# Idle products around the opening transposes, one normalization moved ahead of weight splits, and two tiles' transposes moved inside V

## The chip, the cores and the metric

The kernel runs on one core of a Trainium2 chip. The metric is the time of one execution in microseconds on the device; the time before is the median of three runs. A core has five engines with queues of their own: PE (TensorE, matrix products and transposes), DVE (VectorE), ACT (ScalarE), POOL (GpSimd) and SP (SyncE, which here issues the DMA transfers). Each works through its instructions in order; semaphores tie them together.

## The reference

The program is a block of two layers on x of 2048 rows and 640 columns, in float32. First sliding-window attention with 32 heads of 20, then a gated MLP with a product over the positions:

```python
h = x + _A_ref(_layernorm(x), A_wqkv, A_wo)          # attention, window 256
h2 = h + _B_ref(_layernorm(h), B_w_in, B_w_sp, B_b_sp, B_w_out)
# _A_ref begins with
qkv = (x @ wqkv).reshape(B, S, 3, H, Dh)
```

What matters here is the very beginning: the layer normalization of x and V, the product of normalized x with the 640 columns of wqkv that make v.

## The kernel before

x is cut into 16 tiles of 128 rows (tile 0 to 15). Products are made at about float32 accuracy from operands that are split in two: `hi`, a rounded copy that ACT writes, and `lo`, the rest, `raw - hi`, that DVE or POOL computes. Each product of V is then three: hi·hi, hi·lo and lo·hi.

The kernel opens with the V stage. Its parts, per tile i:

- `load_x(i)`: a DMA of the tile, issued by SP into one of three buffers.
- `ln1(i)` (through `layernorm`, L71 to L83): on DVE the statistics (two at L76, L77, L78), on POOL the reciprocal root as a power (L79), on DVE the normalized tile `xn` (L82). An optional function `between` is called after L79 is issued and before L82, so what it issues on DVE stands between them.
- `turn1(i)`: five transposes on PE (L443), in two banks of PSUM, four and one; ACT copies each bank as hi (L447), DVE subtracts for lo (L448). PSUM banks are taken in turn from a ring of three (`s2_tile`).
- `vgemm(i)`: two halves of 320 columns (j = 0 and 1), in each five steps k of three products (L459, L460, L461), then a copy to `v_sb` on ACT (L462). The profile shows the first half as tile `v`, the second as `bank`; wv's split pieces are `slot` (hi and lo), the transposed x is `xa` (later `xb`).

The weight wv arrives as ten pieces, five for the first 320 columns and five for the other 320, and `split_wv` turns each into hi (ACT, L529) and lo (DVE or POOL, L530). The order of the beginning is written by hand: for DVE, PE and ACT the program's order is the order of execution. It is: `ln1(0)` with the split of the first piece as `between`, splits of the other four pieces of the first half, `turn1(0)`, `ln1(1)`, splits of the second half. Then the loop over tiles: `load_x(i + 3)`, `ln1(i + 2)`, and `vgemm(0)` before `turn1(1)` for i = 0, but `turn1(i + 1)` before `vgemm(i)` for every later i.

After the V stage come the products for q and k, the attention loop, the output projection and the MLP; the change touches none of them.

Of the kernel before, what the change touches and what calls it, by code (L numbers as in the profile page):

```python
# [7 lines left out]
F32 = mybir.dt.float32  # L8
F32R = mybir.dt.float32r
BF16 = mybir.dt.bfloat16  # L10
# [5 lines left out]
P = 128  # L16
# [4 lines left out]
NT = S // P  # L21
KD = D // P
# [12 lines left out]
def block_kernel(ctx, tc, x, wqk, wv, wo, w_in, wsp, bsp, w_out, out):  # L35
    nc = tc.nc
# [4 lines left out]
    def pool(stack, name, **kw):  # L41
        return stack.enter_context(tc.tile_pool(name=name, bufs=1, reuse_waits="tile", **kw))
# [29 lines left out]
    def layernorm(dst, src, n, key, between=None):  # L72
        st, mv = stat_tiles(key)
        hn = n // 2
        for j in range(2):
            nc.vector.bn_stats(out=st[:, j, :], in_=src[:, j * hn:(j + 1) * hn])  # L76
        nc.vector.bn_aggr(out=mv[:, 0:2], in_=st)  # L77
        nc.vector.tensor_scalar(out=mv[:, 2:3], in0=mv[:, 1:2], scalar1=EPS, scalar2=None, op0=OP.add)  # L78
        nc.gpsimd.tensor_tensor(out=mv[:, 3:4], in0=mv[:, 2:3], in1=half, op=OP.pow)  # L79
        if between is not None:  # L80
            between()
        nc.vector.tensor_scalar(out=dst, in0=src, scalar1=mv[:, 0:1], scalar2=mv[:, 3:4],  # L82
                                op0=OP.subtract, op1=OP.mult)  # L83
# [118 lines left out]
    with ExitStack() as ab:  # L202
# [6 lines left out]
        xb = pool(lowx, "xb")  # L209
        xb = [xb.tile([P, CH], F32R, name=f"xb{i}") for i in range(2)]  # L210
# [39 lines left out]
        banks = [ps6.tile([P, 512], F32, name=f"bank{i}") for i in range(6)]  # L250
        ring = {1: banks[2::-1], 2: banks[3:]}

        def s_tile(which):
            ring[which].append(ring[which].pop(0))
            return ring[which][-1]

        def s1_tile():
            return s_tile(1)

        def s2_tile():  # L260
            return s_tile(2)

        def pv_tile(name):
            return psA.tile([P, 512], F32, tag="pv", bufs=2, name=name)
# [158 lines left out]
        if True:  # L423
# [3 lines left out]
            def load_x(i):  # L427
                xts[i] = tmp.tile([P, D], F32, tag="ta", bufs=3, name=f"xt{i}")
                for c in halves if i == 0 else (slice(0, D),):
                    nc.sync.dma_start(xts[i][:, c], x[i * P:(i + 1) * P, c])  # L430

            def ln1(i, between=None):
                xn = tmp.tile([P, D], F32, tag="tb", bufs=2, name=f"xn{i}")
                layernorm(xn, xts.pop(i), D, f"a{i}", between)
                xns[i] = xn

            def turn1(i):
                xn = xns.pop(i)
                c, o = divmod(i, 4)
                for k0, k1 in ((0, 4), (4, KD)):  # L440
                    ps = s2_tile()
                    for k in range(k0, k1):
                        nc.tensor.transpose(ps[:, (k - k0) * P:(k - k0 + 1) * P], xn[:, k * P:(k + 1) * P], ident)  # L443
                    hi = xn_hi[c][:, k0:k1, o * P:(o + 1) * P]
                    lo = xn_lo[c][:, k0:k1, o * P:(o + 1) * P]
                    p3 = ps[:, :(k1 - k0) * P].rearrange("p (k t) -> p k t", k=k1 - k0)
                    nc.scalar.activation(hi, p3, AF.Copy)  # L447
                    nc.vector.tensor_tensor(out=lo, in0=p3, in1=hi.bitcast(F32), op=OP.subtract)  # L448

            def vgemm(i):  # L450
                c, o = divmod(i, 4)
                t0 = o * P
                for j in range(2):
                    ps = s1_tile() if j else pv_tile(f"v{i}_{j}")
                    n0 = j * HD
                    for k in range(KD):
                        hi, lo = xn_hi[c][:, k, t0:t0 + P], xn_lo[c][:, k, t0:t0 + P]
                        wh, wl = wv_hi[:, k, n0:n0 + HD], wv_lo[:, k, n0:n0 + HD]
                        nc.tensor.matmul(ps[:, :HD], hi, wh, start=(k == 0), stop=False)  # L459
                        nc.tensor.matmul(ps[:, :HD], hi, wl, start=False, stop=False)  # L460
                        nc.tensor.matmul(ps[:, :HD], lo, wh, start=False, stop=(k == KD - 1))  # L461
                    nc.scalar.activation(v4[:, i, 16 * j:16 * j + 16, :DH],  # L462
                                         ps[:, :HD].rearrange("p (h c) -> p h c", c=DH), AF.Copy)
# [3 lines left out]
            def load_wqk(m):  # L467
                raws[m] = tmp.tile([P, KD, P], F32, tag="wraw", bufs=4, name=f"wqraw{m}")
                nc.sync.dma_start(raws[m], wqk[m])

            def split_wqk(m):
                raw = raws.pop(m)
                hi = tmp.tile([P, KD, P], F32R, tag="wqh", bufs=4, name=f"wqh{m}")
                lo = tmp.tile([P, KD, P], F32R, tag="wql", bufs=4, name=f"wql{m}")
                nc.scalar.activation(hi, raw, AF.Copy)
                nc.gpsimd.tensor_tensor(out=lo, in0=raw, in1=hi.bitcast(F32), op=OP.subtract)
                wqs[m] = (hi, lo)
# [41 lines left out]
            halves = [slice(0, HD), slice(HD, D)]  # L519
# [8 lines left out]
            def split_wv(k, c, eng):  # L528
                nc.scalar.activation(wv_hi[:, k, c], wv_raw[k][:, c], AF.Copy)  # L529
                eng.tensor_tensor(out=wv_lo[:, k, c], in0=wv_raw[k][:, c], in1=wv_hi[:, k, c].bitcast(F32),  # L530
                                  op=OP.subtract)

            c = halves[0]
            ln1(0, lambda: split_wv(0, c, nc.vector))
            for k in range(1, KD):
                split_wv(k, c, nc.vector if k % 2 == 0 else nc.gpsimd)
            turn1(0)
            ln1(1)
            for k in range(KD):
                split_wv(k, halves[1], nc.gpsimd if k % 2 else nc.vector)  # L540
            for i in range(NT):
                if i + 3 < NT:
                    load_x(i + 3)
                if i + 2 < NT:
                    ln1(i + 2)
                if i == 0:
                    vgemm(0)
                if i + 1 < NT:
                    turn1(i + 1)
                if i >= NT - 6 and i < NT - 2:  # L550
                    load_wqk(i - (NT - 6))
                if i >= NT - 3:
                    split_wqk(i - (NT - 3))
                if i:
                    vgemm(i)
            for j in range(4):
                r = slice(32 * j, 32 * j + 32)
# [646 lines left out]
    n = NT - 2  # L1204
# [34 lines left out]
```

## Time and profile before

| | |
|---|---|
| time before, median of 3 runs | 1129.89 us (1129.07 to 1131.32) |
| the profiled execution, its own time | 1132.75 us |
| its span, first to last instruction | 1130.4 us |
| mean granted TensorE clock over the span | 0.991 |
| 40 slices of the span | 28.3 us each |

The span is what the profile sees; the execution's own time is 2.35 us longer, for what lies around the first and the last instruction. The tables read from left to right: start in us from the span's start, duration, engine, line, operation, written tile <- read tile, and in square brackets how long the engine was idle just before and what ended that. The line numbers are those of the kernel before. The clock column of a stretch is the share of full TensorE clock that was granted, as far as the profile recorded its changes.

### The profile page before, as it was taken

To read this page: it belongs to the slowest core of one execution; us is meant where nothing else is said; L and a number is where in the kernel's file an instruction comes from. 1 tells how busy PE (TensorE), PEld (TensorE's weight loads), DVE (VectorE), ACT (ScalarE), POOL (GpSimd) and SP (SyncE) were. 2 spreads that over 40 slices of the span, in tenths; PEclk is the share of its full clock that TensorE was granted. 3 is DMA by queue.
4 is the path that set the end of the run, shared out by engine and by line. 5 is a ranking of instruction groups with operands and counts; after the bars stand their busy time and mean duration, and the time that the engine had idled before them with its cause. 6 is when DMAs were issued, how large, how long until landed. Compare 5 with 4: busy or idle time off the path is not lost.

```text
span 1130.4 us, 27633 instructions
## 1 busy us (share of the span) xinstructions
PE 1092.4 (97%) x10652; PEld 982.4 (87%) x10652; DVE 739.5 (65%) x2011; ACT 551.1 (49%) x1181; POOL 385.2 (34%) x505
## 2 busy tenths in 40 slices
PE   6999999999999999888999999999999999999998
PEld 6998887668887886788999999999989899999998
DVE  6541222889999997599678478655457974556542
ACT  4333443259999999343366566433336521222210
POOL 3114444457777778365230154000034410000000
PEclk9999999999999999898999999999999999999999
DMA  6212565665666645578555421424341554444331
GB/s 198 70 36 87 167 224 172 199 210 187 220 207 205 205 133 184 169 255 279 207 170 198 152 66 39 137 85 142 118 164 54 170 185 143 124 147 137 109 93 60
DMA packets 84420, 172.61 MB, mean 153 GB/s; under 512 B 11072, under 2 KB 47424, under 8 KB 80448
## 3 DMA queue, kind: packets, MB, share of 16 engines
q1 hardware_dynamic: 81984, 165.60, 45.5%
q10 hardware_dynamic: 2304, 5.24, 1.2%
q8 instruction: 83, 1.36, 0.5%
q14 instruction: 49, 0.40, 0.1%
HBM read 113.25 MB, written 57.11 MB: 151 GB/s over the span
## 4 chain that ended last, share of the span: by engine, by line
PE 72%; DVE 10%; DMA 7%; issue 5%; POOL 4%; SPq 2%; ACT 1%; POOLq 0%; DVEq 0%; ACTq 0%
PE g L1030 20%; PE out_ps L1069 8%; PE pv L395 6%; PE bank L301 5%; PE bank L367 5%; PE wo_ps L92 3%; PE zx L867 2%; PE qk L483 2%; PE qk L485 2%; PE qk L484 2%; PE zv L867 2%; DVE zl L676 2%; DVE aw L676 2%; PE zy L867 1%; POOL sg L502 1%
## 5 line engine op out<-in xcount | busy, mean ns | idle before, releaser
L370 ACT ACTIVATE pt<-bank 128x384 f32<-128x384 f32 (+2 forms) x512 | 200.4, 492 | 9.6 <-PE bank L367 5.0
L1030 PE MATMUL g<-zl,aw 128*128 128x432 f32 x768 | 172.7, 362 | 1.6 <-DVE zl L676 1.3
L682 ACT ACTIVATE aw<-fx 128x512 fp32r<-128x512 f32 (+2 forms) x160 | 92.5, 594 | 156.7 <-PE g L1030 99.4
L313 DVE CUSTOM_DVE_ANT_0 junk<-bank,strip 128x288 bf16<-128x288 f32 x392 | 157.5, 454 | 4.1 <-PE bank L301 1.4
L1030 PEld LDWEIGHTS g<-zl,aw 128*128 128x128 f32 x768 | 144.8, 190 | 9.1 <-DVE zl L676 2.3
L1030 PE MATMUL g<-ze,aw 128*128 128x432 f32 x576 | 134.0, 362 | 4.5 <-DVE row L676 2.5
L395 PE MATMUL pv<-pt,v_sb 128*32 128x192 f32 (+3 forms) x1984 | 127.2, 322 | 3.6 <-POOL pt L372 2.1
L676 DVE TENSOR_TENSOR aw<-fx,aw 128x512 fp32r<-128x512 f32 (+2 forms) x152 | 106.9, 713 | 27.1 <-ACT aw L682 26.3
L1030 PEld LDWEIGHTS g<-ze,aw 128*128 128x128 f32 x576 | 107.1, 188 | 12.4 <-DVE row L676 4.1
L367 PE MATMUL bank<-slot 123*32 123x288 bf16 (+5 forms) x1536 | 106.2, 280 | 1.6 <-ACT pt L370 0.6
L372 POOL TENSOR_SCALAR_AFFINE_SELECT pt<-pt 128x512 f32<-128x512 f32 x128 | 84.4, 659 | 44.9 <-ACT pt L370 44.1
L1069 PE MATMUL out_ps<-wout,y_sp 128*128 128x320 f32 (+1 forms) x630 | 96.2, 309 | 0.4 <-ACT y_sp L125 0.4
L919 PE MATMUL zb<-win,aw 128*128 128x432 f32 x480 | 95.5, 359 | 0.0
L1069 PEld LDWEIGHTS out_ps<-wout,y_sp 128*128 128x128 f32 (+1 forms) x630 | 94.0, 188 | 1.2 <-ACT y_sp L125 0.7
L919 PEld LDWEIGHTS zb<-win,aw 128*128 128x128 f32 x480 | 89.9, 188 | 5.0 <-ACT aw L682 0.4
L301 PE MATMUL bank<-slot 120*32 120x288 bf16 (+2 forms) x1264 | 88.5, 283 | 1.3 <-DVE mcol L313 1.0
L499 DVE TENSOR_TENSOR rest<-qk,sg 128x512 f32<-128x512 f32 x40 | 27.7, 691 | 86.1 <-ACT sg L497 86.0
L375 POOL TENSOR_SCALAR_AFFINE_SELECT pt<-pt 128x512 f32<-128x512 f32 x112 | 72.6, 648 | 0.0
L502 POOL TENSOR_TENSOR sg<-rest,sg 128x512 bf16<-128x512 f32 x40 | 46.6, 1165 | 69.6 <-ACT sg L501 65.8
L395 PEld LDWEIGHTS pv<-pt,v_sb 128*32 128x32 f32 x1984 | 60.0, 110 | 9.5 <-POOL pt L372 4.3
L367 PEld LDWEIGHTS <-slot 123*32 123x32 bf16 x1536 | 53.0, 96 | 16.8 <-issue 5.9
L676 DVE TENSOR_TENSOR row<-g,row 128x432 f32<-128x432 f32 x80 | 47.9, 602 | 29.4 <-PE g L1030 24.1
(190 smaller groups left out, 2169.4 us busy)
## 6 DMA issues: line engine op xcount, KB each, us to landing
fx<-wsp_in SPq DMA_DIRECT2D x32, 512.0 KB
slot<-qk_d SPq DMA_DIRECT2D x72, 200.0 KB
qk_d<-sg SPq DMA_DIRECT2D x32, 384.0 KB
slot<-qk_d SPq DMA_DIRECT2D x72, 160.0 KB
fx<-hn_d SPq DMA_DIRECT2D x32, 320.0 KB
o_d<-ot SPq DMA_DIRECT2D x64, 128.0 KB
z_d<-row SPq DMA_DIRECT2D x18, 432.0 KB
g_d<-row SPq DMA_DIRECT2D x16, 432.0 KB
```

The lines of the kernel that those rows point to most:

```text
L301: nc.tensor.matmul(ps[32 * j:32 * j + 32, :n], part(st, half, 120, 0, hh, q0, 32), part(st, half, 120, 1, hh, lo + skip * j, n), start=Tru ...
L313: nc.vector.tensor_tensor_reduce(out=junk[:, :n], in0=ps[:, :n], in1=keep, scale=1.0, scalar=NEG, op0=OP.add, op1=OP.max, accum_out=m_cols ...
L367: nc.tensor.matmul(ps[32 * i:32 * i + 32, b:e], part(st, half, 123, 1, hh, k0, 32), part(st, half, 123, 0, hh, kb * P + b, e - b), start=T ...
L370: nc.scalar.activation(pt[:, hh, :n], ps[:, :n], AF.Exp, scale=SCALE)
L372: nc.gpsimd.affine_select(out=pt[:, :, :P], in_=pt[:, :, :P], pattern=[[0, 4], [1, P]], base=0, channel_multiplier=-1, compare_op=OP.is_ge ...
L375: nc.gpsimd.affine_select(out=pt[:, :, 256:], in_=pt[:, :, 256:], pattern=[[0, 4], [-1, P]], base=-1, channel_multiplier=1, compare_op=OP. ...
L395: nc.tensor.matmul(ps[32 * hh:32 * hh + 32, a - 512 * c:b - 512 * c], v_sb[:, kb, v0:v0 + 32], pt[:, hh, a - kb * P:b - kb * P], start=fir ...
L676: (eng or nc.vector).tensor_tensor(out=out, in0=a, in1=b, op=op)
L682: nc.scalar.activation(out, a, AF.Copy)
L919: nc.tensor.matmul(b[0][:, :HF], a[t][:, x, kk], win2[0][:, y, kk, h * HF:(h + 1) * HF], start=kk + x + y == 0, stop=kk == KD - 1 and x == 1)
L1030: nc.tensor.matmul(ps, w[m][:, x, k], zc[k][m][:, y], start=start and k + x + y == 0, stop=stop and k == 3 and x == 1, skip_group_check=True)
L1069: nc.tensor.matmul(ps[j][:, :HD], src[:w, a, k, :], e1["wout"][:w, b, k, j * HD:(j + 1) * HD], start=(k == 0 and a + b == 0), stop=(k == K ...
```

## The change

Four things are done.

1. At the start DVE fills a piece of `xb[1]`, not yet in use, with ones, and PE runs 11 products of 128 x 512 on it into `banks[0]`; four more follow `turn1(0)`. Nobody reads their result.
2. `ln1(0)` is issued whole before any split, and `turn1(0)` stands after the third of the first half's five pieces, not after the fifth.
3. In `ln1(1)` the first two pieces of wv's second half are split between the power and the normalization; on DVE that is one remainder ahead of `xn` of tile 1 and two behind.
4. `vgemm` gets a parameter `middle`, called in its second half before step k = 3. For i = 0 and 1 the transposes `turn1(i + 1)` stand there, and `ln1(i + 2)` follows behind `vgemm(i)`. From i = 2 on the loop is as before.

```diff
+        idle = xb[1][:, :256].bitcast(F32)
+        nc.vector.memset(idle, 1.0)
+        idle = idle.bitcast(BF16)
+
+        def idle_products(n):
+            for _ in range(n):
+                nc.tensor.matmul(banks[0], idle[:, :P], idle, start=True, stop=True)
+
+        idle_products(11)
...
-            def vgemm(i):
+            def vgemm(i, js=(0, 1), middle=None):
                 c, o = divmod(i, 4)
                 t0 = o * P
-                for j in range(2):
+                for j in js:
                     ps = s1_tile() if j else pv_tile(f"v{i}_{j}")
                     n0 = j * HD
                     for k in range(KD):
+                        if middle is not None and (j, k) == (1, 3):
+                            middle()
...
-            c = halves[0]
-            ln1(0, lambda: split_wv(0, c, nc.vector))
-            for k in range(1, KD):
-                split_wv(k, c, nc.vector if k % 2 == 0 else nc.gpsimd)
+            def split_half(c, ks):
+                for k in ks:
+                    split_wv(k, c, nc.gpsimd if k % 2 else nc.vector)
+
+            ln1(0)
+            split_half(halves[0], range(3))
             turn1(0)
-            ln1(1)
-            for k in range(KD):
-                split_wv(k, halves[1], nc.gpsimd if k % 2 else nc.vector)
+            idle_products(4)
+            split_half(halves[0], range(3, KD))
+            ln1(1, lambda: split_half(halves[1], range(2)))
+            split_half(halves[1], range(2, KD))
             for i in range(NT):
                 if i + 3 < NT:
                     load_x(i + 3)
+                if i < 2:
+                    vgemm(i, middle=lambda: turn1(i + 1))
                 if i + 2 < NT:
                     ln1(i + 2)
-                if i == 0:
-                    vgemm(0)
-                if i + 1 < NT:
+                if 1 < i < NT - 1:
                     turn1(i + 1)
...
-                if i:
+                if i > 1:
                     vgemm(i)
```

How that moves VectorE's rows, from the normalization of tile 1 to that of tile 3. The digit behind a name is the tile or the piece (`xn1`, `wvraw2`); `slot0_1` is lo of wv, L448 writes lo of the transposed tile. Before:

```order
L82 TENSOR_SCALAR xn1_179<-xt1_141,mva1_181 128x640
L530 TENSOR_TENSOR slot0_1_101<-wvraw0_131,slot0_0_100 128x320
L530 TENSOR_TENSOR slot0_1_101<-wvraw2_133,slot0_0_100 128x320
L530 TENSOR_TENSOR slot0_1_101<-wvraw4_135,slot0_0_100 128x320
L76 BN_STATS sta2_201<-xt2_148 128x6 x2
L77 BN_AGGR mva2_202<-sta2_201 128x2
L78 TENSOR_SCALAR mva2_202<-mva2_202 128x1
L82 TENSOR_SCALAR xn2_200<-xt2_148,mva2_202 128x640
L448 TENSOR_TENSOR xa_91<-bank5_124,xa_91 128x4x128
L448 TENSOR_TENSOR xa_91<-bank3_122,xa_91 128x128
L76 BN_STATS sta3_254<-xt3_198 128x6 x2
```

And with the change, the same engine and stretch:

```order
L542 TENSOR_TENSOR slot0_1_101<-wvraw0_143,slot0_0_100 128x320
L82 TENSOR_SCALAR xn1_195<-xt1_153,mva1_197 128x640
L542 TENSOR_TENSOR slot0_1_101<-wvraw2_145,slot0_0_100 128x320
L542 TENSOR_TENSOR slot0_1_101<-wvraw4_147,slot0_0_100 128x320
L458 TENSOR_TENSOR xa_91<-bank5_124,xa_91 128x4x128
L458 TENSOR_TENSOR xa_91<-bank3_122,xa_91 128x128
L76 BN_STATS sta2_259<-xt2_160 128x6 x2
L77 BN_AGGR mva2_260<-sta2_259 128x2
L78 TENSOR_SCALAR mva2_260<-mva2_260 128x1
L82 TENSOR_SCALAR xn2_258<-xt2_160,mva2_260 128x640
L458 TENSOR_TENSOR xa_91<-bank4_123,xa_91 128x4x128
L458 TENSOR_TENSOR xa_91<-bank5_124,xa_91 128x128
```

The first remainder of the second half moved ahead of `xn1`, and the statistics of tile 2, which stood ahead of tile 1's two subtractions, now stand behind them; those of tile 3 stand behind tile 2's as before, but tile 2's subtractions are now issued from inside V of tile 1. The row after the last is the statistics of tile 3.

On PE, the end of V of tile 1 (`bank1`) and what follows it. Before:

```order
L460 MATMUL bank1_120<-slot0_1_101,xa_91 128x320
L461 MATMUL bank1_120<-slot0_0_100,xa_91 128x320
L443 MATMUL bank3_122<-ident_73,xn3_253 128x128 x4
L443 MATMUL bank4_123<-ident_73,xn3_253 128x128
L459 MATMUL v2_0_324<-slot0_0_100,xa_91 128x320
```

With the change:

```order
L473 MATMUL bank1_120<-slot0_0_100,xa_91 128x320
L453 MATMUL bank4_123<-ident_73,xn2_258 128x128 x4
L453 MATMUL bank5_124<-ident_73,xn2_258 128x128
L471 MATMUL bank1_120<-slot0_0_100,xa_91 128x320
L472 MATMUL bank1_120<-slot0_1_101,xa_91 128x320
L473 MATMUL bank1_120<-slot0_0_100,xa_91 128x320
L471 MATMUL bank1_120<-slot0_0_100,xa_91 128x320
L472 MATMUL bank1_120<-slot0_1_101,xa_91 128x320
L473 MATMUL bank1_120<-slot0_0_100,xa_91 128x320
L453 MATMUL bank3_122<-ident_73,xn3_311 128x128 x4
L453 MATMUL bank4_123<-ident_73,xn3_311 128x128
L471 MATMUL v2_0_340<-slot0_0_100,xa_91 128x320
```

The transposes of tile 2 moved from ahead of V of tile 1 to six products before its end; those of tile 3 stand where they stood, between V of tile 1 and V of tile 2.

## The prediction

> **What bounds the kernel now.** I read the page first (engine totals and the chain that ended last), then the timeline of the opening microseconds, then the same chain in order of time, then clock and busy time in stretches around TensorE's longest waits.
>
> From the page, busy time and the chain's shares:
>
> ```profile
> PE 1092.4 (97%) x10652; PEld 982.4 (87%) x10652; DVE 739.5 (65%) x2011; ACT 551.1 (49%) x1181; POOL 385.2 (34%) x505
> PE 72%; DVE 10%; DMA 7%; issue 5%; POOL 4%; SPq 2%; ACT 1%; POOLq 0%; DVEq 0%; ACTq 0%
> ```
>
> TensorE is the bound and the program is one long chain. The change touches only its first 30 us, so I ask one question: when does the even rhythm of the V stage begin, before and after? What that moment gains or loses goes through to the end. I call V0, V1, V2 the 30 products of tiles 0, 1, 2, and A and B the two halves of wv's columns.
>
> The opening, from the timeline (start, duration, engine, line, what, in brackets the idle time ahead and its releaser):
>
> ```profile
> 0.80 0.20 POOL L60 MEMSET ident<- 128x128 f32 x1 [0.29 <-POOLq L1231]
> 1.86 1.14 POOL L243 MEMSET v_sb<- 128x512 f32 x1
> 4.60 0.57 POOL L79 TENSOR_TENSOR mva<-mva,half 128x1 f32<-128x1 f32 x1 [0.27 <-DVE mva L78]
> 5.19 1.32 ACT L529 ACTIVATE slot<-wvraw 128x320 fp32r<-128x320 f32 x3 [3.11 <-DMA wvraw<-wv_in]
> 5.69 0.49 DVE L530 TENSOR_TENSOR slot<-wvraw,slot 128x320 fp32r<-128x320 f32 x1 [1.17 <-ACT slot L529]
> 6.10 1.27 DVE L82 TENSOR_SCALAR xn<-xt,mva 128x640 f32<-128x640 f32 x1
> 7.43 1.33 PE L443 MATMUL bank<-ident,xn 128*128 128x128 f32 x5 [7.43 <-DVE xn L82]
> 8.58 0.77 ACT L447 ACTIVATE xa<-bank 128x512 fp32r<-128x512 f32 x2 [0.54 <-PE bank L443]
> 9.23 0.64 PE L459 MATMUL v<-slot,xa 128*128 128x320 f32 x1 [0.47 <-ACT xa L447]
> 9.45 2.23 ACT L529 ACTIVATE slot<-wvraw 128x320 fp32r<-128x320 f32 x5
> 10.01 0.88 DVE L76 BATCH_NORM_STATS2 sta<-xt 128x6 f32<-128x320 f32 x2
> 10.43 1.77 POOL L530 TENSOR_TENSOR slot<-wvraw,slot 128x320 fp32r<-128x320 f32 x2 [1.94 <-ACT slot L529]
> 12.16 0.56 POOL L79 TENSOR_TENSOR mva<-mva,half 128x1 f32<-128x1 f32 x1
> 12.75 0.61 DVE L82 TENSOR_SCALAR xn<-xt,mva 128x640 f32<-128x640 f32 x1 [1.43 <-POOL mva L79]
> 13.28 1.29 DVE L530 TENSOR_TENSOR slot<-wvraw,slot 128x320 fp32r<-128x320 f32 x3
> 16.46 0.61 DVE L82 TENSOR_SCALAR xn<-xt,mva 128x640 f32<-128x640 f32 x1 [0.66 <-POOL mva L79]
> 18.29 0.33 PE L443 MATMUL bank<-ident,xn 128*128 128x128 f32 x1 [0.51 <-DVE xa L448]
> ```
>
> And the chain that ended last, in order of time:
>
> ```profile
> 11.92 0.27 PE v L461
> 12.72 0.27 PE v L461
> 15.56 0.15 PE bank L459
> 17.55 0.70 DVE xa L448
> 23.03 0.55 PE bank L443 x5
> 27.98 0.55 PE bank L443 x5
> ```
>
> A 320-column product costs 0.267 us at 12 ((12.72 - 11.92)/3) and 0.15 at 15.6: TensorE starts at half clock and doubles inside V0. (The clock column reads 1.00 there, so at the start the pitch is the witness.) Yet V1's start is not set by that: the second tile's transposes wait for xn2, normalized at 16.46 to 17.07, and end with the one at 18.29. So the slow products of V0 are largely hidden behind VectorE. The rhythm is reached at 23.03, tile 3's transposes; from there a tile takes 27.98 - 23.03 = 4.95 us with TensorE never waiting, 0.55 for the transposes and 0.147 for each of 30 products. **23.03 is the mark.**
>
> **Part by part.** *Memset and 11 products.* VectorE is idle until x lands. A 128x256 fill lies between the fills of 0.20 and 1.14 us, so TensorE starts near 1.1 to 2. A 512-column product is 0.27 x 512/320 = 0.43 us slow (an estimate), eleven 4.7, over by about 5.9 to 6.7. The stretch was empty; cost nothing, at most 0.8 where they run into tile 0's transposes, and the B pieces below hide that too.
>
> *Normalization first.* rstd ends at 5.17, so xn0 runs at about 5.2 to 5.8 instead of 6.10 to 7.37; its transposes start 1.5 us sooner. ScalarE then copies after the third A piece (6.51), not after the fifth: 0.61 more, and V0 starts at about 7.3 (8.7 if the four idle products still run slow) instead of 9.23. That is 0.5 to 1.9 us of head start on TensorE, and at full speed 0.12 us on each slow product.
>
> *What is late next.* The B half. SP's timeline, and its waits in the same stretch:
>
> ```profile
> 9.10 0.33 SPq L430 DMA_DIRECT2D xt<-x_in  x1
> SPq L469 <- DMA wvraw<-wv_in: 0.4, 1, 0.4
> ```
>
> SP's issue at 9.10 waits for x1, its next one for the first two B pieces, and goes on waiting for them to 9.43 + 0.4 = 9.83. ScalarE used the first at 9.45, so the second lands at 9.83; before, ScalarE reached it at 9.45 + 2.23/5 = 9.90. Starting earlier thus buys 0.07 us. Behind it all stays as it was: POOL's two remainders end at 12.13, the power at 12.65, xn1 at 13.3. In the new order one of VectorE's three B remainders goes ahead of xn1 (where VectorE idled 1.43 us), so the piece k = 2 ends at 13.3 - 0.07 + 1.29/3 = 13.65. V0's 23rd product needs it. TensorE, at full speed, has done the 15 products of the A half by about 9.8; the first B remainder follows the statistics of x1 (landed by 9.1; 0.88 and two short ones, some 1.3, and the remainder 0.43), so TensorE waits a microsecond for it, to about 10.9, and six products later, at 11.7, is at the 23rd. So V0 stands still about 2.0 us, and tile 1's transposes come at 13.65 + 0.1 + 2 x 0.15 = 14.05.
>
> *Transposes inside V.* From a steady tile, what follows transposes that start at 27.98:
>
> ```profile
> 28.45 0.77 ACT L447 ACTIVATE xa<-bank 128x512 fp32r<-128x512 f32 x2
> 29.09 0.89 DVE L448 TENSOR_TENSOR xa<-bank,xa 128x512 fp32r<-128x512 f32 x2 [1.35 <-ACT xa L447]
> 29.89 0.87 DVE L76 BATCH_NORM_STATS2 sta<-xt 128x6 f32<-128x320 f32 x2
> 31.93 0.61 DVE L82 TENSOR_SCALAR xn<-xt,mva 128x640 f32<-128x640 f32 x1 [0.73 <-POOL mva L79]
> ```
>
> VectorE's low part starts 1.11 us after the transposes, and the normalization queued behind it ends 31.93 + 0.61 - 27.98 = 4.56 after them. In V1 that is covered: V0's last six products end at 14.05 + 0.55 + 0.88 = 15.5, V1's third waits for the low part till 14.05 + 1.11 + 0.70 + 0.06 = 15.9, 22 more take 3.23, so tile 2's transposes come at 19.15, with xn2 ready at 18.6. But xn3 now stands behind tile 2's low part on VectorE: ready at 19.15 + 4.56 + 0.06 = 23.77. V1 ends at 19.15 + 0.55 + 0.88 = 20.6, and tile 3's transposes stand ahead of V2. **TensorE waits 3.2 us there, and the mark moves from 23.03 to 23.77: 0.7 us later**, whatever the clock did in V0. If the B pieces cost VectorE nothing beyond ScalarE's earliest order (pieces from 8.2 rather than 9.45), the same sum gives 0.5 us earlier; that is the favourable end.
>
> *The two waits.* What TensorE's clock does after waits, in stretches (start:end, length, busy time of PE, PEld, DVE, ACT, POOL, granted clock, DMA):
>
> ```profile
> 460.20:464.23 4.03, 0.00 (x1) 0.00 (x1) 2.47 (x4) 0.00 (x0) 0.09 (x1) 0.68 0.43 130
> 490.76:492.14 1.38, 0.00 (x0) 0.03 (x1) 1.38 (x4) 0.56 (x1) 0.80 (x1) 1.00 1.05 373
> 492.14:495.80 3.66, 3.66 (x25) 3.66 (x26) 3.66 (x7) 1.46 (x3) 3.12 (x4) 1.00 0.91 304
> 496.63:499.24 2.61, 0.00 (x1) 0.03 (x1) 2.61 (x4) 1.30 (x2) 2.12 (x3) 0.99 0.40 151
> 499.24:502.62 3.38, 3.38 (x14) 3.31 (x15) 3.35 (x7) 1.80 (x5) 2.40 (x3) 0.50 0.75 249
> 517.47:520.37 2.90, 0.01 (x2) 0.04 (x1) 2.90 (x6) 1.19 (x2) 1.32 (x2) 0.88 0.92 234
> 520.37:526.50 6.13, 6.13 (x23) 6.13 (x24) 6.13 (x10) 1.47 (x3) 4.34 (x4) 0.50 0.72 228
> 834.99:836.82 1.83, 0.00 (x1) 0.00 (x1) 1.74 (x4) 0.33 (x1) 1.01 (x1) 1.00 0.62 252
> 836.82:840.54 3.72, 3.72 (x11) 3.43 (x12) 2.79 (x4) 2.74 (x6) 1.75 (x2) 0.54 0.23 66
> ```
>
> A wait of 1.38 us left the clock at 1.00; waits of 1.83, 2.61, 2.90 and 4.03 were followed, or overtaken, by half clock, and 3.4 to 6.1 us of work then ran at 0.50. A slow microsecond loses 1 - 0.147/0.267 = 0.45 us, so such a stretch costs 1.5 to 2.75. The new wait of 3.2 us ahead of V2 lies between 2.90 and 4.03: I take the drop, and the mean of the three quoted stretches, (3.38 + 6.13 + 3.72)/3 = 4.4 us, x 0.45 = 2.0. V0's wait of 2.0, with one microsecond shortly ahead of it, lies between 1.83 and 2.61: I take the drop there too, at the lower price, 1.5, since V1 then runs slow right up to a wait that would come anyway.
>
> The Trainium skill ("TensorE: Matmul & The Clock Gate", section "HAM oscillation — how this bites in real kernels") says the clock drops in idle gaps above about 3.4 us. By that rule neither wait drops it and the sum is 0.7 alone. The rows with 1.83 and 2.61 speak against the rule as a threshold. The same page (Part 1) has a free-running window of 3413 ns; the drops read from the clock shares above (461.65, 499.2, 519.7, 837.1) lie 11, 6 and 93 such windows apart, which agrees.
>
> **Sum:** 0.7 + 1.5 + 2.0 = 4.2 us later. The profiled execution took 1132.75 us (span 1130.4 and 2.35 around it) and would take about 1137.0; the median of the runs is 2.86 below it, so 1129.89 + 4.2 = 1134.1.
>
> **Rivals.** *Both waits, no drop:* only the moved chain counts, 1129.89 + 0.7 = 1130.6. For it: both waits are shorter than the 4.03 in which the drop is seen whole inside a wait. Against: four drops in four waits from 1.83 up. Chance 0.09.
>
> *One drop only:* 0.7 + 1.5 = 2.2 or 0.7 + 2.0 = 2.7, so 1132.1 to 1132.6. It happens if TensorE reaches the 23rd product later than I think, so that V0's wait falls under 1.4. Chance 0.20, half of it on each side of 0.2%.
>
> *Faster, because TensorE's time decides after all:* V0 from 7.3 at full speed, no wait for B pieces beyond 10.9, V1 and V2 right behind. V0 and its transposes end at about 12.9, V1 and its own at 17.9, so tile 3's transposes come at 17.9 instead of 23.03: 1124.8. It turns faster by 0.2% only where xn3 is ready by 20.8 and no clock drops. VectorE's order speaks against it: xn3 cannot come sooner than 4.56 + 5.1 after tile 1's transposes, and these need a piece that passes POOL and VectorE late. Chance 0.04.
>
> *The change doesn't do what it says:* the idle products leave the clock at half. V0 then runs from 8.7 at 0.27, reaches tile 1's transposes at 8.7 + 24 x 0.27 = 15.2 without the wait, 1.1 us later than above, and V1 runs partly slow: 0.7 + 1.1 + 2.0 and up to 1.5 more, 1133.7 to 1135.2. Against it: the products and transposes make some 7 us of nearly unbroken work, where V0's own work, from 9.23, brought full speed somewhere between 13.0 and 15.6. Chance 0.07.
>
> **How the numbers follow.** The forecast, both drops, has 0.60, with a range of its own from 0.7 + 1.5 + 1.5 to 0.7 + 2.75 + 2.75, 1133.6 to 1136.1. A measurement of this kernel can tell about 0.2%, 2.3 us, from no change. Slower: 0.60 + 0.10 + 0.07 = 0.77; within: 0.10 + 0.09 = 0.19; faster 0.04. The range takes in one drop, no drop down to the run spread, and 0.4 above the costliest: 1130.4 to 1136.5.
>
> **What would show it.** Right: xn0 near 5.2, V0 from about 7.3 at a pitch of 0.147, TensorE idle about 2 us before V0's 23rd product and about 3.2 us before tile 3's transposes, clock 0.50 in V1 and again in V2, and the mark later than 23.03. Wrong: xn1 well before 13.3; xn3 ready while V1 still runs; clock 1.00 through V2; or the pitch of 0.27 still in V0.

## The result, and the profile after

| | before | with the change |
|---|---|---|
| median beside each other, 4 runs each | 1130.61 us | 1137.30 us (1137.19 to 1139.94) |
| ratio, 95% interval | | 1.0052 [1.0027, 1.0077] |
| the profiled execution, its own time | 1132.75 us | 1139.94 us |
| its span | 1130.4 us | 1138.2 us |
| tile 3's transposes, the mark | 23.03 | 24.42 |
| tile 4's transposes | 27.98 | 31.13 |
| first product for q and k | 91.6 | 94.8 |

The changed kernel is slower, by 6.7 us in this comparison. The last two rows say how much of that the trace puts at the place of the change: about 3.2 us.

The opening with the change, from the timeline (columns as before the prediction):

```profile
1.25 4.34 PE L259 MATMUL bank<-xb 128*128 128x512 bf16 x11 [1.25 <-DVE xb L254]
5.22 0.61 DVE L82 TENSOR_SCALAR xn<-xt,mva 128x640 f32<-128x640 f32 x1 [0.69 <-POOL mva L79]
7.23 0.43 PE L471 MATMUL v<-slot,xa 128*128 128x320 f32 x1
9.41 2.23 ACT L541 ACTIVATE slot<-wvraw 128x320 fp32r<-128x320 f32 x5 [1.34 <-DMA wvraw<-wv_in]
10.40 1.88 POOL L542 TENSOR_TENSOR slot<-wvraw,slot 128x320 fp32r<-128x320 f32 x2 [1.74 <-ACT slot L541]
12.83 0.61 DVE L82 TENSOR_SCALAR xn<-xt,mva 128x640 f32<-128x640 f32 x1 [2.10 <-POOL mva L79]
13.90 0.41 PE L472 MATMUL bank<-slot,xa 128*128 128x320 f32 x1 [1.67 <-DVE slot L542]
361.39 0.28 PE L311 MATMUL bank<-xb 120*32 120x256 bf16 x1 [1.80 <-issue]
```

The first row is the idle products, the second tile 0's normalization, 0.9 us earlier than before (6.10); V0 starts at 7.23 instead of 9.23. Two microseconds are won there, and then ScalarE waits for wv's second half until 9.41 (before 9.45): the transfers set what follows. TensorE stands 1.67 us for a remainder of wv, and tile 1's normalization ends at 13.44, where it ended before (12.75 + 0.61 = 13.36). The last row belongs to another stage and is used further down.

The chain that ended last, in order of time:

```profile
13.36 0.50 DVE slot L542
13.90 0.41 PE bank L472
14.46 0.45 PE bank L453 x4
16.31 0.41 PE v L473
19.81 0.45 PE bank L453 x4
20.91 0.89 DVE xa L458 x2
21.80 0.80 DVE sta L76 x2
23.76 0.62 DVE xn L82
24.42 0.77 PE bank L453 x5
31.13 0.55 PE bank L453 x5
```

The first two rows are the remainder of wv that TensorE waits for and the product that uses it. The transposes of tiles 1, 2, 3 and 4 stand at 14.46, 19.81, 24.42 and 31.13. Between tile 2's and tile 3's the chain leaves TensorE: tile 2's low part (L458), then the statistics and normalization of tile 3, all on VectorE but for the power. From 31.13 on the rhythm of 4.95 us is reached.

The clock around that wait, in stretches of one microsecond:

```profile
17.00:18.00 1.00, 1.00 (x9) 1.00 (x8) 0.61 (x3) 0.00 (x0) 0.24 (x1) 1.00 0.27 105
22.00:23.00 1.00, 0.00 (x0) 0.00 (x0) 0.93 (x4) 0.00 (x0) 0.00 (x0) 1.00 0.02 8
25.00:26.00 1.00, 1.00 (x7) 1.00 (x6) 0.53 (x3) 0.77 (x2) 0.26 (x1) 0.70 0.60 195
28.00:29.00 1.00, 1.00 (x6) 1.00 (x5) 0.90 (x4) 0.04 (x1) 0.00 (x0) 0.59 0.83 233
29.00:30.00 1.00, 1.00 (x9) 1.00 (x8) 0.30 (x1) 0.40 (x1) 0.55 (x1) 1.00 0.20 77
```

Full clock in V1 (17 to 18), an empty TensorE at 22 to 23, half clock from about 25.4 to 28.8 in V2, full clock again. The stage thus loses 24.42 - 23.03 = 1.39 up to the mark, and (31.13 - 24.42) - 4.95 = 1.76 in the tile behind it: 3.15 together. Of the 1.76, the half clock makes 3.4 x 0.45 = 1.5, and the transposes behind the wait, 0.77 instead of 0.55, the other 0.2. The start of the q and k products shows the same sum; these are the first row's first and last start of the line, before and with the change:

```profile
L483 PE MATMUL qk<-xa,wqh x100: 392/395/534, 91.6 to 206.6; 128*128 128x512 f32 x100
```

```profile
L495 PE MATMUL qk<-xa,wqh x100: 392/392/534, 94.8 to 210.5; 128*128 128x512 f32 x100
```

94.8 - 91.6 = 3.2. The spans differ by 7.8, so 4.6 us of that lie behind the V stage, in work that the change doesn't touch and whose instructions stand in the same order.

### The profile page after: what moved, and what is told of

It reads as the page before. It is cut to its first block, busy times and chain, and to the rows that moved or that the text cites. A ratio compares the mean times of both kernels' runs of the same rounds, so it can differ in the third digit from the quotient of the medians.

```text
span 1138.2 us, 27666 instructions
## 1 busy us (share of the span) xinstructions
PE 1096.9 (96%) x10667; PEld 984.0 (86%) x10667; DVE 737.6 (65%) x2012; ACT 552.1 (49%) x1181; POOL 386.8 (34%) x505
## 3 DMA queue, kind: packets, MB, share of 16 engines
q8 instruction: 84, 1.38, 0.5%
## 4 chain that ended last, share of the span: by engine, by line
PE 72%; DVE 9%; DMA 6%; issue 5%; POOL 4%; ACT 2%; SPq 2%; POOLq 0%; ACTq 0%; DVEq 0%
PE g L1045 22%; PE out_ps L1084 8%; PE pv L405 6%; PE bank L377 5%; PE bank L311 5%; PE wo_ps L92 3%; PE zx L882 2%; PE qk L495 2%; PE qk L497 2%; PE qk L496 2%; PE zv L882 2%; DMA qk_d<-sg 2%; DVE zl L691 2%; PE zy L882 1%; POOL sg L514 1%
## 5 line engine op out<-in xcount | busy, mean ns | idle before, releaser
L691 DVE TENSOR_TENSOR aw<-fx,aw 128x512 fp32r<-128x512 f32 (+2 forms) x152 | 104.0, 694 | 26.7 <-ACT aw L697 20.4
L934 PEld LDWEIGHTS zb<-win,aw 128*128 128x128 f32 x480 | 90.6, 189 | 4.7
```

Of the source, the lines that this page charges most:

```text
L691: (eng or nc.vector).tensor_tensor(out=out, in0=a, in1=b, op=op)
L934: nc.tensor.matmul(b[0][:, :HF], a[t][:, x, kk], win2[0][:, y, kk, h * HF:(h + 1) * HF], start=kk + x + y == 0, stop=kk == KD - 1 and x == 1)
```

## The experiments

Two questions. First, what of the loss belongs to the change at all: the 3.2 us of the V stage, or all 6.7. Second, what in the V stage does it: the transposes inside V (part 4), the idle products (part 1), or the order of splits and normalization (parts 2 and 3). Each kernel was timed beside runs of the kernel before; the three sets, each on a chip of its own, had medians of that of 1133.14 us (22 runs; again, gapfill, allmid, noidle), 1132.17 (29; before2, nomid, mid2, mid2_noidle) and 1132.21 (29; mid2_late, idleonly, midonly). "Rest" is the span less the start of the q and k products.

| kernel | tile 3's transposes | tile 4's | q, k start | span | rest | median, us | ratio to before [95%] |
|---|---|---|---|---|---|---|---|
| before | 23.03 | 27.98 | 91.6 | 1130.4 | 1038.8 | | |
| before2 | 22.50 | 27.46 | 91.1 | 1132.7 | 1041.6 | | |
| the change | 24.42 | 31.13 | 94.8 | 1138.2 | 1043.4 | 1137.30 | 1.0052 [1.0027, 1.0077] |
| again | 24.41 | 31.12 | 94.8 | 1135.7 | 1040.9 | 1137.49 | 1.0028 [1.0011, 1.0045] |
| gapfill | 24.51 | 29.69 | 93.3 | 1139.2 | 1045.9 | 1137.72 | 1.0029 [1.0010, 1.0048] |
| allmid | 25.21 | 30.55 | 95.6 | 1135.2 | 1039.6 | 1137.34 | 1.0043 [1.0019, 1.0067] |
| noidle | 24.70 | 32.61 | 96.3 | 1132.7 | 1036.4 | 1135.00 | 1.0019 [1.0000, 1.0038] |
| nomid | 22.23 | 27.19 | 90.8 | 1130.5 | 1039.7 | 1133.47 | 1.0010 [0.9992, 1.0027] |
| mid2 | 24.93 | 29.88 | 91.5 | 1132.7 | 1041.2 | 1132.39 | 0.9999 [0.9981, 1.0017] |
| mid2_noidle | 23.93 | 28.89 | 90.6 | 1130.5 | 1039.9 | 1130.42 | 0.9981 [0.9958, 1.0004] |
| mid2_late | 23.64 | 28.59 | 89.1 | 1128.6 | 1039.5 | 1130.88 | 0.9988 [0.9969, 1.0008] |
| idleonly | 24.58 | 29.53 | 93.2 | 1137.4 | 1044.2 | 1133.53 | 1.0013 [0.9989, 1.0036] |
| midonly | 25.84 | 32.28 | 95.9 | 1134.4 | 1038.5 | 1137.66 | 1.0047 [1.0028, 1.0066] |

Where transposes stand inside V for every tile (allmid and the mid2 kernels) they come before a tile's last products, not behind them, so there only the start of q and k compares with the others.

### again: the changed kernel once more

No edit.

> The changed kernel itself once more, beside the kernel before on one chip. The V stage should again be about 3 us late from tile 4 on (31.13 against 27.98 in the profiles), by xn3 and the clock. Theory A: the other 3 to 4 us of the +6.7 are later in the program and belong to the change (places of its instruction stream, or transfers met at another moment); they come again, ratio about 1.006. Theory B: they are an accident of single executions; ratio about 1.003.

Its trace, in the timeline:

```profile
24.41 0.77 PE L453 MATMUL bank<-ident,xn 128*128 128x128 f32 x5 [3.19 <-DVE xn L82]
```

The wait of 3.19 us, the mark and the slow tile repeat to 0.01 us. The span does not: 1135.7 against 1138.2, all of it behind the V stage (rest 1040.9 against 1043.4). In medians the change costs 1137.49 - 1133.14 = 4.35 us here, by its ratio of 1.0028 it costs 3.2.

### before2: the kernel before once more

No edit; a single profile, to see the rest of one kernel twice.

> The kernel before once more, for a second trace. If the part behind the V stage varies by itself, its length (span less the start of the q and k products, 1038.8 us in the first profile) differs by some microseconds with the V stage alike to 0.3 us (mark 23.0, tile 4's transposes 28.0, V's end 91.2), as it did for the changed kernel (1043.4 and 1040.9). If it is stable, 1038 to 1039.5 again.

The V stage was 0.5 us earlier (22.50, 27.46), the rest 2.8 us longer: 1041.6 against 1038.8. So 2.5 and 2.8 us separate two traces of one kernel behind the V stage, and all 13 traces lie between 1036.4 and 1045.9 there, with no relation to where the V stage ended: the shortest rest is that of noidle, whose V stage ended last. The reading that all 6.7 us are the change's falls; 3.2 are by the first trace of the kernel before, 3.7 by the second (94.8 - 91.1), and spread can make the remainder of the first comparison. Most of it comes in the attention: from the start of the q and k products to the end of the last product into `pv`, the traces of before, before2, the change and again took 379.4, 384.7, 383.6 and 380.8 us. What makes it is open. Over the 80 timed executions of the kernel before, the longer ones tend to have the lower mean clock (correlation -0.64), but the clock alone is not it: again has a mean of 0.995 and noidle 0.989, and noidle's rest is 4.5 us shorter. The row at 361.39 above is one place in one trace: TensorE idle 1.80 us, "issue", for nothing that the profile shows.

### gapfill: fill the wait ahead of V2

```diff
+                if i == 2:
+                    idle_products(13)
                 if 1 < i < NT - 1:
                     turn1(i + 1)
```

> 13 more idle products between V of tile 1 and the transposes of tile 3, where TensorE waits 3.2 us. If the wait drops the clock (my theory), V of tile 2 now runs at a pitch of 0.147 throughout, the mark (tile 3's transposes) stays at about 24.4 and tile 4's transposes come at about 29.4 instead of 31.1: 1.5 to 2 us faster than the changed kernel. If the slow stretch has another cause, V of tile 2 is slow as before and the time is the changed kernel's or up to 2 us more.

From the timeline, and from the chain:

```profile
21.16 2.98 PE L259 MATMUL bank<-xb 128*128 128x512 bf16 x13
24.51 0.77 PE L453 MATMUL bank<-ident,xn 128*128 128x128 f32 x5 [0.37 <-DVE xn L82]
```

```profile
29.69 0.55 PE bank L453 x5
```

The mark stays (24.51), since VectorE sets it. But TensorE is busy for all but 0.37 us of the wait, and tile 4's transposes follow 5.18 us later instead of 6.71. That the lost clock cost 1.53 us is thereby shown. The q and k products start 1.5 us sooner than with the change. The median says nothing of it (1137.72): this trace has the longest rest of all, 1045.9.

### noidle: without the idle products

```diff
-        idle_products(11)
...
-            idle_products(4)
```

> The changed kernel without the 15 idle products. My theory: V of tile 0 runs at half clock from about 7.3, is at its 23rd product at about 13.5 and waits there only some 0.4 us, so tile 1's transposes come at the same 14.3 and the mark at the same 24.4 (up to 25 if V of tile 1 begins slow): within 1 us of the changed kernel, with no clock drop in V of tile 0. Rival (the idle products carry the opening): the mark comes 2 us or more later, 1139 or more. If the lengths of the later stages hang on the places of PE's instructions, the later 3 to 4 us may be gone, since 30 instructions are.

The chain in order of time:

```profile
13.35 0.27 PE bank L471
13.84 0.15 PE bank L470
14.73 0.45 PE bank L452 x4
32.61 0.55 PE bank L452 x5
```

V0 runs at a pitch of 0.27 and doubles by itself before 13.84. That it is slow is hidden: tile 1's transposes come at 14.73 instead of 14.46, the mark at 24.70 instead of 24.42. Fifteen products that speed up all of V0 buy 0.3 us. The wait of 3.19 us is the same; here the clock drops inside it, so that the five transposes take 1.33 and tile 4's follow only 7.91 us later. The half pitch lasts to 30.8, and the drop costs 7.91 - 4.95 = 2.96 us. The median is nevertheless lower than that of the change (1135.00 against 1137.49); the two intervals overlap, and this trace has the shortest rest of all. The timeline's row:

```profile
24.70 1.33 PE L452 MATMUL bank<-ident,xn 128*128 128x128 f32 x5 [3.19 <-DVE xn L82]
```

### nomid: parts 1 to 3 without part 4

The changed kernel with the loop over tiles of the kernel before:

```diff
-                if i < 2:
-                    vgemm(i, middle=lambda: turn1(i + 1))
                 if i + 2 < NT:
                     ln1(i + 2)
-                if 1 < i < NT - 1:
+                if i == 0:
+                    vgemm(0)
+                if i + 1 < NT:
                     turn1(i + 1)
...
-                if i > 1:
+                if i:
                     vgemm(i)
```

> The changed kernel with its fourth part undone: transposes of every tile ahead of V of the tile before, as in the kernel before; idle products and the moved normalization stay. My theory: xn1 is at 13.4 as always, tile 2's normalization follows the B remainders at once (14.3 + 2.6 = 16.9) instead of behind tile 1's subtractions, so the mark (tile 3's transposes) is at 22.4 to 23.1 instead of 24.4, with no 3.2 us wait and no slow V of tile 2: tile 4's transposes at about 27.4 to 28 instead of 31.1, about the kernel before's 27.98. Rival (the new opening itself costs): the mark stays at 24 or later.

```profile
22.23 0.55 PE bank L453 x5
27.19 0.55 PE bank L453 x5
```

In its chain the mark is at 22.23 and the period 4.96, full clock throughout: 0.3 to 0.8 us ahead of the two traces of the kernel before (23.03, 22.50), and 1.0010 [0.9992, 1.0027] in time. Parts 1 to 3 do no harm together; the loss is part 4's.

### midonly: part 4 alone

The kernel before with `middle` in `vgemm` and the changed loop, nothing else.

> The kernel before with the fourth part alone (transposes of tiles 1 and 2 inside V of tiles 0 and 1, normalizations behind). V of tile 0 at half clock from 9.1; tile 1's transposes at 14.8 to 15.3, tile 2's 5.35 later, tile 3's 4.6 after those: mark at 24.7 to 25.3, after a TensorE wait of 3.2 us; then V of tile 2 at half clock for 3.4 us or more, tile 4's transposes at 31.4 to 33 instead of 27.5 to 28. My theory: 3.5 to 5 us slower than before, at least as much as the whole change. Rival (the fourth part hides transposes and gains by itself): mark not later than 23.

Timeline and chain:

```profile
25.84 1.33 PE L443 MATMUL bank<-ident,xn 128*128 128x128 f32 x5 [3.19 <-DVE xn L82]
```

```profile
32.28 0.55 PE bank L443 x5
```

The same wait of 3.19 us, the same slow tile (6.44 from mark to tile 4's transposes), q and k 4.3 us later than in the first trace of before: the whole loss and more, 1.0047 in time.

### idleonly: part 1 alone

The kernel before with the memset, the 11 products and the 4.

> The kernel before with the memset and the 11 + 4 idle products alone. My theory: they cannot help, since V of tile 1 waits for xn2 on VectorE; V of tile 0 runs at full clock, has done the first half by 11.5 and then waits about 2 us for the first remainder of wv's second half (13.7). Mark at 22.5 to 23.1 as in the two traces of before if the clock holds over that wait, up to 24.5 if it drops: 0 to 1.5 us slower than before. Rival (the slow clock of the opening is what bounds before): mark 1 us or more earlier than 22.5.

Its timeline, a stretch of one microsecond, and its chain:

```profile
14.14 0.46 PE L470 MATMUL bank<-slot,xa 128*128 128x320 f32 x1 [2.44 <-DVE slot L540]
```

```profile
15.00:16.00 1.00, 1.00 (x6) 1.00 (x5) 0.93 (x4) 0.00 (x0) 0.00 (x0) 0.50 0.82 238
```

```profile
24.58 0.55 PE bank L453 x5
```

In the old order the idle products make V0's first half fast enough to meet the second half's remainder 2.44 us too early. Right behind that wait, at 14.4, the clock drops, and V0's second half runs at half speed after all, now later: the mark is 24.58, 1.5 to 2.1 us behind the kernel before. There the slow clock of V0 was hidden behind VectorE, and the slow products filled that wait.

### allmid: the transposes inside V for every tile

```diff
-                if i < 2:
+                if i + 1 < NT:
                     vgemm(i, middle=lambda: turn1(i + 1))
...
-                if 1 < i < NT - 1:
-                    turn1(i + 1)
...
-                if i > 1:
+                if i + 1 == NT:
                     vgemm(i)
```

> Transposes of every tile i + 1 inside V of tile i, with the next normalization behind it. VectorE's chain from transposes to the next xn is 4.6 us, a tile on TensorE 4.95, so no wait ahead of any transposes; tile 4's transposes at about 14.3 + 5.3 + 2 x 4.95 + 4.95 = 34.5 inside V of tile 3, which is V of tile 3 starting at about 25.9 instead of 31.7 in the changed kernel and 28.5 before. My theory (the switch back to transposes ahead of V is what costs): 5 us faster than the changed kernel in the V stage, 2.5 to 3 faster than before. Rival (something else in the new opening costs): no faster than before.

The chain, and what its timeline shows of V2:

```profile
25.21 0.45 PE bank L453 x4
30.55 0.45 PE bank L453 x4
```

```profile
26.62 0.30 PE L472 MATMUL v<-slot,xa 128*128 128x320 f32 x1
27.06 0.41 PE L473 MATMUL v<-slot,xa 128*128 128x320 f32 x1
```

The expected period of 4.95 us did not come. The wait of 3.2 us and the clock drop are gone, as they should be where no step from one order to the other is left, but the period is 5.34: six products (0.88 us) stand between the transposes and the next V, and the third product of V, the first that reads the low part, starts 27.06 - 26.62 = 0.44 us after the second instead of 0.15 and itself costs more, as one behind a wait does (below). A small loss in each of 15 tiles costs more than the one large one: q and k start at 95.6.

### mid2, mid2_noidle, mid2_late: the transposes one step earlier

All three are allmid with nine products behind the transposes instead of six. The second is also without the idle products. The third is the second with the first two of the three splits of the q and k weights, which sit in the last three tiles of the loop, moved one tile on.

```diff
-                        if middle is not None and (j, k) == (1, 3):
+                        if middle is not None and (j, k) == (1, 2):
                             middle()
```

```diff
-                if i >= NT - 3:
-                    split_wqk(i - (NT - 3))
+                if i >= NT - 2:
+                    for m in ((0,), (1, 2))[i - (NT - 2)]:
+                        split_wqk(m)
```

> As allmid, but the transposes stand before step k = 2 of the second half, so that nine products (1.32 us) instead of six (0.88) stand between them and V of the next tile. In allmid a tile took 5.34 us instead of 4.95, because its third product waits 0.36 us for the low part. If that wait is the whole of it, the period is 4.95 again, tile 2's V starts at about 20.5 (before: 23.57) and V ends about 3 us before the kernel before's 91.2; total 3 us faster than before, about 0.997. Rival (VectorE's chain of 4.6 us cannot keep up with 4.95 in the long run): period stays over 5.2 and no gain.

> mid2 without the 15 idle products. V of tile 0 at half clock from 8.5 is at its 22nd product at about 14.1, where xn1 has been ready since 13.4: tile 1's transposes 0.5 to 0.7 us later than in mid2, all else the same; V ends 0.5 to 1 us later than in mid2. If the idle products are what wins, 2 us or more later.

> mid2_noidle with the first of wq/wk's splits one tile later, so that POOL's 1.58 us remainder no longer stands ahead of the power of tile 15, for which TensorE waited 0.9 us before tile 15's transposes (84.23 instead of 83.34). V ends at about 89.2 instead of 90.1 (91.2 and 90.7 in the two traces of before); in all 1.5 to 2 us faster than before, ratio 0.998 to 0.9985 by the V stage, with some 0.002 of spread from the part behind it. Rival: the q and k products now wait for the split that comes later (start of q and k more than 0.6 us behind the end of V), no gain over mid2_noidle.

Of mid2 two waits in the timeline, a stretch of half a microsecond, and the chain:

```profile
11.38 0.42 PE L472 MATMUL bank<-slot,xa 128*128 128x320 f32 x1 [0.66 <-DVE slot L542]
13.27 0.82 PE L453 MATMUL bank<-ident,xn 128*128 128x128 f32 x5 [0.88 <-DVE xn L82]
```

```profile
13.50:14.00 0.50, 0.50 (x6) 0.50 (x5) 0.50 (x2) 0.04 (x1) 0.00 (x0) 0.85 0.95 379
```

```profile
13.27 0.82 PE bank L453 x5
19.98 0.55 PE bank L453 x5
24.93 0.55 PE bank L453 x5
```

Nine products are cover enough: 24.93 - 19.98 = 4.95, no wait. But the first step takes 6.71: two short waits were followed by half clock from 13.85, and what the order won was given back. The chain of mid2_noidle:

```profile
13.93 0.64 PE bank L452 x5
18.98 0.55 PE bank L452 x5
```

Without idle products V0 runs slow through the same stretch, arrives when its inputs do, and no clock is lost: 13.93 to 18.98 in 5.05, then 4.95. mid2_noidle loses 0.89 us once, late in the stage:

```profile
84.23 0.77 PE L452 MATMUL bank<-ident,xn 128*128 128x128 f32 x5 [0.89 <-DVE xn L82]
```

There a weight split stood ahead of tile 15's power on POOL; mid2_late moves it, and q and k start at 89.1, 2.0 to 2.5 us ahead of the kernel before and 5.7 ahead of the changed one. In time it is 0.9988 [0.9969, 1.0008] of before: its interval lies below that of the change, but against the kernel before the interval takes in no difference, and only the traces show the gain.

## Why the prediction was right or wrong

The sign was right, and so was the mechanism ahead of V2; one of the two clock drops did not come. The measured 1137.30 is 3.2 us above the 1134.1 of the forecast and 0.8 above the end of its range. But the kernel before also took 1130.61 beside it, not the 1129.89 that the forecast started from: the ratio of 1.0052 on 1129.89 gives 1135.8, 1.7 above the forecast and inside the range. That it comes so near is partly luck, since the V stage lost 3.15 of the 4.2 forecast, and what came on top of it lies where the sum has no term. The sum, step by step:

- **The opening: right.** xn0 at 5.22 (5.2 to 5.8 said), V0 from 7.23 (7.3) at full speed, and nothing of the two microseconds left by tile 1's normalization: ready at 13.44 (13.3), because ScalarE stood for wv's second half until 9.41. noidle and nomid confirm it from two sides: without the fast V0 the new order's mark moves by 0.3, and with parts 1 to 3 the old order's moves by 0.3 to 0.8.
- **The mark: right in kind, half the size.** 0.7 was said, 1.39 came. Tile 1's transposes stood at 14.46 instead of 14.05: the remainder ended at 13.86, not 13.65, and the product behind that wait took 0.41 us in the chain where the sum had counted 0.15. The same was missed in V1: its third product waited for the low part until 16.31, 1.85 after the transposes (said: 1.11 + 0.70 + 0.06 = 1.87), and again took 0.41 and not 0.15, so tile 2's transposes stood 5.35 behind tile 1's, not 5.10. From there to the mark 4.61 came for the 4.62 said.
- **The wait of 3.2 us ahead of V2: right, to 0.01 in two traces,** and with the cause named: tile 3's normalization behind tile 2's low part on VectorE. midonly has the same 3.19 with part 4 alone, and nomid has no wait ahead of tile 3's transposes.
- **The clock lost in that wait: right.** 2.0 was said, for 4.4 us at half clock; 1.76 came, 1.5 of it for 3.4 us at half clock and 0.2 for slower transposes behind the wait. gapfill takes 1.53 back by filling the wait.
- **The clock lost in V0's wait: wrong.** Here is the step that failed: "I take the drop there too, at the lower price, 1.5". The wait was 1.67 and not 2.0 us, because the 23rd product's turn came later than assumed, and V1 ran at full clock, in the trace of the change and in those of again, gapfill, allmid and nomid, whose V0 waits were 1.67 to 1.69. The rival with one drop was the case that happened, though not by its condition, a wait under 1.4: V stage 1.39 + 0 + 1.76 = 3.15 against the 4.2 of the forecast. The step took the length of a single wait for what decides; the rows on the clock below show that it doesn't.
- **The time: too low for another reason.** With 3.15 on the median before the sum would have given 1133.0. What was measured above that is no loss that the V stage shows, and spread behind it, for which the sum had no term and the range 0.4 us, is the reading that fits: the kernel before alone ran from 1127.87 to 1138.53 in the three sets. In the set of again the difference of the medians was 4.35 us, [1.2, 5.1] by its ratio's interval ([1.0011, 1.0045] of 1133.14), and that takes in 3.15; the interval of the first comparison, [3.1, 8.7] us, just does.
- **A rival's arithmetic.** In the case "faster", V0 and its transposes end not at 12.9 but at 11.7 + 8 x 0.147 + 0.55 = 13.4 by the prediction's own prices, so its time is 1125.2 and not 1124.8.

On the clock, the later traces show more than the four waits that the prediction had. Half clock followed TensorE waits of 1.76 (mid2), 1.83, 2.44, 2.61 and 2.90 us and all of 3 us and more; full clock stayed over waits of 1.38 and 1.67 to 1.69, but also over one of 1.80 (the row at 361.39), of 2.16 (noidle, 839.03 to 841.19) and of 2.86 us (again). The Trainium skill ("TensorE: Matmul & The Clock Gate", section "HAM oscillation — how this bites in real kernels") puts the drop at idle gaps above about 3.4 us; these rows disagree. And mid2 dropped after 0.66 and 0.88 us, so the length of a single wait does not decide.

What fits is the busy share of a fixed stretch of time. In all 13 traces the recorded changes of the clock lie on a grid of 3.413 us, exact to about 0.001 us, which stands at another place against the start of each trace; half clock lasts one or two steps of it. Two such steps of again, around its wait of 2.86 us (501.91 to 504.78), then two of the change, around the wait of 2.87 ahead of the same transposes, which belong to a later stage (504.26 to 507.13), then the steps of the change that hold V0's wait and most of the one ahead of V2 (start:end, length, busy time of PE, PEld, DVE, ACT, POOL, granted clock, DMA):

```profile
500.29:503.70 3.41, 1.62 (x12) 1.36 (x10) 2.62 (x2) 1.66 (x3) 3.03 (x2) 1.00 0.74 196
503.70:507.11 3.41, 1.90 (x13) 1.74 (x14) 3.38 (x8) 1.47 (x4) 1.93 (x2) 1.00 0.57 120
```

```profile
503.27:506.68 3.41, 0.99 (x7) 0.73 (x5) 3.41 (x3) 1.54 (x3) 2.41 (x2) 1.00 0.67 209
506.68:510.09 3.41, 2.96 (x12) 2.92 (x13) 3.38 (x8) 1.59 (x5) 1.96 (x3) 0.50 0.50 74
11.75:15.16 3.41, 1.74 (x13) 1.46 (x13) 1.41 (x3) 0.44 (x2) 1.04 (x2) 1.00 0.79 261
21.99:25.40 3.41, 0.98 (x8) 0.98 (x9) 2.58 (x8) 0.28 (x1) 0.55 (x1) 1.00 0.03 8
```

In again the edge of a step divides the wait, TensorE is busy for 1.62 and 1.90 of 3.41 us, and the clock stays; in the change one step holds most of it, TensorE is busy for 0.99, and the next step runs at half clock. V0's wait left 1.74, 51% of its step, and kept the clock; the wait ahead of V2 left 0.98. Of the steps that ran at full clock in the 13 traces, all 59 in which TensorE was busy for less than 47% were followed by half clock, none of the 4102 above 60%, and 10 of the 50 between. V0's wait lies in that band, and so does mid2's step from 10.44 to 13.85, 1.87 busy, which was followed by half clock: that V0 kept it in five traces is nothing to count on. Behind these drops, full clock came back after a half-clock step with TensorE busy for over 81%, and never after one with less than 80%; noidle's first one had 2.61 of 3.41, 76%, and so it lost two steps. (At the start of four traces a step with 86% did not bring full clock yet.) No run varied the share by itself, and what decides within the band stays open.

## What to carry to other kernels

A step that is moved on one engine takes along what its results trigger on the others: transposes pulled forward on TensorE put their low part ahead of the next tile's normalization on VectorE, and at the place where the new order changes back to the old one the whole length of that chain lies open, once. Moving all tiles removes that step and shows the next limit, the cover between a product's operands and its first use; count it in products (six were too few by 0.4 us, nine enough). And work that brings the clock up early is worth nothing, or less, where inputs arrive late: TensorE then only reaches its wait sooner, and can lose the clock by it, as in idleonly.

## What the hardware showed that I had not expected

- Where a wait lies on the clock's grid of 3.413 us counts as much as its length: one of 2.44 us in idleonly and two of 0.66 and 0.88 in mid2 were enough for half clock, while one of 2.86 in again left it full. A step of the grid at half clock cost 1.5 us (1.53 in gapfill, 6.44 - 4.95 = 1.49 in midonly), two cost 3.0 in noidle.
- The first product behind a wait took 0.41 us in the chain instead of 0.15 (13.90, 16.31), and the five transposes behind one 0.77 instead of 0.55 at the same full clock (24.51 in gapfill): these waits cost some 0.2 us more than their length.
- The profile's clock column reads 1.00 at the start of the kernel before and of noidle, where the pitch of 0.267 us shows half speed. Before the first recorded change only the pitch tells.
- Two traces of the changed kernel agree to 0.01 us at the marks of the first 31 us and differ by 2.5 us behind; the two of the kernel before differ by 0.5 and 2.8 us; over all traces the untouched part took 1036.4 to 1045.9 us. An edit worth 3 us is judged better here by the trace of its own stage than by a handful of times. What makes the spread stays open.
